# Dealing matmuls out between attention's last steps, a relu part on another engine, and the parts of x2 behind their transposes

## The chip, the core and the metric

The kernel runs on one core of a Trainium2 chip. The metric is the device time of one execution in microseconds (us), the median of several runs. A core has five engines, each with its own in-order queue: TensorE (PE: matmuls and transposes), VectorE (DVE), ScalarE (ACT), GpSimd (POOL) and SyncE (SP, which here only issues DMAs). An instruction that waits holds up all that stands behind it on its engine.

## The reference

Three stages in a row, attention with the 32 largest scores, a dense mixture of four experts, and a layer that takes the largest of three products:

```python
scores = q @ k.T / sqrt(64)                    # 2 batches x 8 heads, 576 x 576, float32
mask = scores >= 32nd largest of each row
x = softmax(where(mask, scores, -1e9)) @ v     # then heads side by side: 1152 x 512
p = domain_probs / (domain_probs.sum(-1) + 1e-9)
x = sum over e of p[:, e] * (relu(x @ w1[e]) @ w2[e])       # 4 experts, 512 -> 1024 -> 512
h = max(x @ m1, x @ m2, x @ m3)                # 512 -> 768, weights given as float64
out = h @ w_out                                # 768 -> 512, weights float64
```

## The kernel before

**Products.** A float32 product is made of three faster ones: each operand is split into a high and a low part (`whi`, `wlo` of a weight, `xh`, `xl` of x, `h` and its low part of a hidden layer, `x2h`, `x2l` of the experts' output), and `product` (L682 to L684) adds high by low, high by high and low by high. ACT makes the high part of a weight (L273), POOL or DVE the low part (L279). Tiles are 128 tokens, nine in all.

**Attention** runs in 36 pairs (two heads by 128 tokens), eight steps to a pair. DVE's search for the 32 largest sets its pace. Within a pair, PE transposes the probabilities (`psp`, L491 and L496), ACT copies them (`pt`, L494 and L499), PE multiplies them with v (`psv`, L533 and L536) and transposes the reciprocal sums (`psr`, L519). `attention()` is a generator: it emits one step and yields.

**Dealing out.** The loop at the end of the kernel takes the steps one by one. Each step raises `clock["dve"]` by the time that its DVE work is estimated at, and `clock["goal"]` follows. While `clock["pe"]` is below the goal, `advance()` emits a piece of the next product (`products()`). So products stand between the steps in as large a number as the estimates say. After the last step `attention()` goes on yielding empty steps, each worth `PAUSE` = 0.8, until all conversions are done.

**Conversions.** The float64 weights of the last layer are turned into float32 in 48 pieces (`to_float32`): SP loads a piece (L222), ACT does two operations (L239, L240), DVE three (L242, L244, L246), POOL one (L249), and ACT issues a DMA that writes it to DRAM (L255, tile `narrow`). One begins per two steps from step 306 on (`W_FROM`, `W_STEP`). Four pieces make one float32 weight, which SP loads later (L212, `raw<-narrow`).

**Experts** run in stages 0 to 8, each over two or three tiles and half of the experts' weights. For each expert half, `half1(c, i, u)` makes the hidden layer, and then `half2` of the half before multiplies it into the output. Stage 6 has tiles 5 and 6, stage 7 has 6, 7 and 8, stage 8 has 7 and 8. The evacuation of a hidden layer is the relu on ACT (L824) and the low part on DVE (L826); every fourth one (`ON_POOL_H`) is instead copied by ACT twice (L817, L818), with the low part on POOL (L819). Evacuations are not emitted at once: `later()` puts them on a list, whose next entry `tick()` emits at the next product, and `flush()` empties the list.

**The last layer** (`largest`) follows for three groups of three tiles. `turned` transposes a tile of the experts' output on PE (`pst`, L902), ACT makes `x2h` (L908) and DVE `x2l` (L909), two parts for each tile. Nine `c` products follow (three triples; the largest of a triple is collected in `tm`: L947 on ACT, L949 on DVE; its high part is `hh`, L952 on ACT), then the next group's transposes and the `d` products (`pso`). Hidden layers, `c` products and transposes share six PSUM banks in turn, so each waits until the bank's last tile is evacuated.

Of the kernel before, what the change touches and what calls it, by code (L numbers as in the profile page):

```python
# [24 lines left out]
ON_POOL_H = 4  # L25
# [4 lines left out]
PAUSE = 0.8  # L30
LATE = 7
# [29 lines left out]
def kernel(  # L61
# [41 lines left out]
    HALVES = [range(E) if not n % 2 else range(E, 2 * E) for n in range(len(STAGES))]  # L103
# [24 lines left out]
    clock = {"dve": 0.0, "pe": 0.0, "goal": AHEAD}  # L128
# [4 lines left out]
    def pe(n):  # L133
        clock["pe"] += n / 2400.0

    def bank(name):
        return pg.tile([P, 512], F32, tag="g", name=name)
# [147 lines left out]
    def weight(key, oldest=None):  # L285

        w_split_to(w_index[oldest or key] + W_AHEAD + 2 * whole(key))
        return w_hl[key]
# [90 lines left out]
    def xs_of(tiles):  # L379

        at_ = [place(t) for t in tiles]
        step = max(1, at_[-1] - at_[0]) // max(1, len(at_) - 1)
        assert at_ == list(range(at_[0], at_[-1] + 1, step))
        return [[x[:, a].rearrange("p (s n) -> p s n", n=P)[:, at_[0]:at_[-1] + 1:step] for a in range(KT)] for x in xring]
# [174 lines left out]
    def attention():  # L559

        NP = len(pairs)
# [76 lines left out]
        s = min(later)  # L638
        while s <= end:
            todo = later.pop(s, [])  # L640
            i = 0
            while i < len(todo):
                f, a = todo[i]
                f(*a)
                todo[i + 1:i + 1] = between.pop(s, [])
                todo += later.pop(s, [])
                i += 1
            yield s, [c for c in last if last[c] + (READY if c[1] == HP - 2 else 0) == s]
            s += 1

# [13 lines left out]
    def tick():  # L664
        for x in list(lag):
            x.pop(0)()
            if not x:
                lag.remove(x)

    def flush():  # L670
        while lag:
            tick()

    def later(*stages):
        tick()
        lag.append(list(stages))
# [37 lines left out]
    def hidden(N):  # L714
        if 2 * N <= 512:
            ht = hp_.tile([P, 2, 512], F32R, tag="h", bufs=4, name="h")
            return ht[:, 0, 0:2 * N], ht[:, 1, 0:2 * N]

        assert len(x_ready) == len(pairs) and 2 * N <= 2 * WIDTH
        hh = kv.tile([P, 2, S], F32R, tag="kT", bufs=5, name="hh")  # L720
        hl = hp_.tile([P, 2, 512], F32R, tag="h", bufs=4, name="hl")
        return [x.rearrange("p a n -> p (a n)")[:, 0:2 * N] for x in (hh, hl)]
# [68 lines left out]
    def experts():  # L791
        begin = {}

        def half1(c, i, u):
            tiles = STAGES[c]
            N = len(tiles) * P
            if c in WHOLE:
                ps = bank("ps1")
                w = weight((c, "a", i, u)).rearrange("p (a f) -> p a f", f=256)
                for f in range(2):  # L800
                    for a in range(KT):
                        pe(4 * P)
                        nc.tensor.matmul(ps[:, f * P:(f + 1) * P], lhsT=w[:, a, f * P:(f + 1) * P], rhs=xfull[:, a, :], start=f == a == 0, stop=f == 1 and a == KT - 1)
                    yield True
                h = hp_.tile([P, 2, 512], F32, tag="h", bufs=4, name="hfull")[:, 0, 0:2 * P]
                later(lambda: [nc.scalar.activation(out=h, in_=ps[:, 0:2 * P], func=AF.Relu), made.add(("h", c, i, u))])
                yield h
                return
            for groups in layer1(weight((c, "a", i, u)), xs_of(tiles), N, begin.pop((c, i, u), None)):
                if groups is None:  # L810
                    tick()
                    yield True
            hh, hl = hidden(N)
            count = made_h[0] = made_h[0] + 1
            if ON_POOL_H and not count % ON_POOL_H and (c, i) < (LATE - 1, HALVES[LATE - 1][-1]):
                raw = ms.tile([P, 2 * WIDTH], F32, tag="tm", bufs=2, name="raw")
                later(lambda: [nc.scalar.activation(out=raw[:, g], in_=ps, func=AF.Relu) for g, ps in groups],  # L817
                      lambda: [nc.scalar.activation(out=hh[:, 0:2 * N], in_=raw[:, 0:2 * N], func=AF.Copy),  # L818
                               nc.gpsimd.tensor_tensor(out=hl[:, 0:2 * N], in0=raw[:, 0:2 * N], in1=hh[:, 0:2 * N].bitcast(F32), op=ALU.subtract),  # L819
                               made.add(("h", c, i, u))])  # L820
                yield hh, hl
                return
            dve(2 * N)
            later(lambda: [nc.scalar.activation(out=hh[:, g], in_=ps, func=AF.Relu) for g, ps in groups],  # L824
                  *[lambda: None] * H_LAG,
                  lambda: [nc.vector.scalar_tensor_tensor(out=hl[:, g], in0=ps, scalar=0.0, in1=hh[:, g].bitcast(F32),  # L826
                                                          op0=ALU.max, op1=ALU.subtract) for g, ps in groups]
                  + [made.add(("h", c, i, u))])
            yield hh, hl

        outs = {}

        def half2(c, i, hs, ti):
            t = STAGES[c][ti]
            if not i % 2:
                outs[t] = po.tile([P, DM], F32, tag="o", name="ps2") if ti < 2 else bank("ps2")
            ps = outs[t]
            assert {("h", c, i, 0), ("h", c, i, 1)} <= made
            if c in WHOLE:
                for u in range(2):  # L840
                    w = weight((c, "b", i, u), (c, "b", i, 0)).rearrange("p (f n) -> p f n", f=2)
                    for f in range(2):
                        pe(4 * DM)
                        nc.tensor.matmul(ps, lhsT=hs[u][:, f * P:(f + 1) * P], rhs=w[:, f, :], start=not i % 2 and u == f == 0, stop=i % 2 == 1 and u == f == 1)
                        yield True
            else:
                yield from layer2(ps, [weight((c, "b", i, u), (c, "b", i, 0)) for u in range(2)], hs, len(STAGES[c]) * P, ti, not i % 2, i % 2 == 1)
            if not i % 2:
                return
            first = t not in accs  # L850
            if first:
                sums(t)
            later(*[lambda: None] * E_LAG, gated(ps, t, i // 2, first, c == LAST_IN[t] and i == HALVES[c][-1]))

        before = None
        for c in range(1, len(STAGES)):
            phase[0] = c
            newest = max(STAGES[c])
            if c == 1:
                i = HALVES[c][0]  # L860
                for parts in (range(HP - 2), (HP - 2,)):
                    while (newest, parts[-1]) not in x_ready:
                        yield None
                    for n, x in enumerate([(i, 0), (i, 1), (i + 1, 0), (i + 1, 1)]):
                        if not parts[0]:
                            begin[(c, *x)] = (po if n < 2 else pg).tile([P, 512], F32, tag="go"[n < 2], name="ps1")
                        yield from begun(begin[(c, *x)], weight((c, "a", *x), (c, "a", i, 0)), xs_of(STAGES[c]), 2 * P, parts)
                        flush()
            while (newest, HP - 1) not in x_ready:
                yield None  # L870
            for i in HALVES[c]:
                hs = []
                for u in range(2):
                    for y in half1(c, i, u):
                        if y is not True:
                            hs.append(y)
                        yield True
                if i == HALVES[c][-1]:
                    x_free.update(t for t in STAGES[c] if LAST_IN[t] == c)
                if before is not None:  # L880
                    for ti in range(len(STAGES[before[0]])):
                        yield from half2(*before, ti)
                before = c, i, hs
        flush()
        yield from turned_ahead(len(STAGES))
        for ti in range(len(STAGES[before[0]])):
            yield from half2(*before, ti)
        flush()
# [23 lines left out]
    def turned_ahead(n):  # L912

        if n < len(PHASES) and PHASES[n][0] == 2:
            c = PHASES[n][1]
            for ti in range(len(GROUPS[c])):
                turned(c, ti)
                yield True
# [163 lines left out]
```

## Time and profile before

| | us |
|---|---|
| median of 3 runs | 752.82 (751.12 to 754.62) |
| profiled execution | 751.61 |
| its span (what the trace covers) | 749.5 |
| around the span | 2.1 |
| PE busy | 721.0 |
| DVE busy | 586.7 |
| ACT busy | 505.2 |
| POOL busy | 474.7 |

The granted TensorE clock is at its full level over the whole span. Times in the rows below are us from the start of the span. In the trace attention ends at about 448, the experts at about 592, and the `c` products of the first group run from there to about 631.

### The profile page before, as it was taken

The numbers are of one execution on the slowest core, as the hardware profiler recorded it, in microseconds if no ns is written. First come the engines' busy times: TensorE is split into PE (matmuls) and PEld (weight loads), VectorE is DVE, ScalarE is ACT, GpSimd is POOL, SyncE is SP. The second block draws the span as 40 slices with busy tenths as digits, with TensorE's granted clock in tenths as the row PEclk, the third lists the DMA queues.
The fourth block names the chain that finished last, engine by engine and source line by source line (L and its number), as shares of the span: only waits on it lengthen the run. The fifth ranks groups of instructions, "written<-read, shape, count | busy, mean of one in ns | idle before, by whom it ended". The sixth has DMA issues, their size and how long they took to land. (4 is left out here: it accounts for less than half of the span.)

```text
span 749.5 us, 13764 instructions
## 1 busy us (share of the span) xinstructions
PE 721.0 (96%) x4758; PEld 641.2 (86%) x4758; DVE 586.7 (78%) x1171; ACT 505.2 (67%) x1132; POOL 474.7 (63%) x421
## 2 busy tenths in 40 slices
PE   6799999999999999999999998999999999999997
PEld 4587788888989989898989977899989899999996
DVE  6999989989999899999999965887688754233331
ACT  4668889899977787788797857666557533442531
POOL 2514778689979797697778659875655563442520
PEclk9999999999999999999999999999999999999999
DMA  7594565545647364445445355887879762453501
GB/s 220 179 267 160 154 179 160 156 127 162 190 123 214 109 189 125 148 134 154 142 125 152 126 183 160 299 297 269 293 230 343 245 194 73 153 170 101 195 1 42
DMA packets 56485, 130.15 MB, mean 174 GB/s; under 512 B 9760, under 2 KB 23328, under 8 KB 56416
## 3 DMA queue, kind: packets, MB, share of 16 engines
q1 hardware_dynamic: 48064, 120.69, 51.9%
q10 hardware_dynamic: 8352, 8.59, 3.2%
q8 instruction: 37, 0.61, 0.3%
q14 instruction: 32, 0.26, 0.1%
HBM read 120.60 MB, written 8.65 MB: 172 GB/s over the span
## 5 line engine op out<-in xcount | busy, mean ns | idle before, releaser
L279 POOL TENSOR_TENSOR wlo<-raw,whi 128x512 fp32r<-128x512 f32 x252 | 329.8, 1338 | 126.5 <-ACT whi L273 119.2
L273 ACT ACTIVATE whi<-raw 128x1024 fp32r<-128x1024 f32 x164 | 169.8, 1056 | 29.5 <-issue 9.4
L682 PE MATMUL ps<-xl,whi 128*128 128x256 f32 (+1 forms) x584 | 173.6, 297 | 1.2 <-DVE narrow L246 0.8
L684 PE MATMUL ps<-xh,wlo 128*128 128x256 f32 (+1 forms) x584 | 170.7, 292 | 0.0
L683 PE MATMUL ps<-xh,whi 128*128 128x256 f32 (+1 forms) x584 | 170.6, 292 | 0.0
L445 DVE MAX8 m<-work 128x8 f32<-128x576 f32 x216 | 155.0, 744 | 0.1
L682 PEld LDWEIGHTS ps<-xl,whi 128*128 128x128 f32 x584 | 110.8, 190 | 2.5 <-DVE narrow L246 1.1
L279 DVE TENSOR_TENSOR wlo<-raw,whi 128x1024 fp32r<-128x1024 f32 x38 | 60.4, 1590 | 64.8 <-ACT whi L273 51.9
L683 PEld LDWEIGHTS ps<-xh,whi 128*128 128x128 f32 x584 | 109.8, 188 | 0.8 <-issue 0.2
L684 PEld LDWEIGHTS ps<-xh,wlo 128*128 128x128 f32 x584 | 109.7, 188 | 0.0
L447 DVE MATCH_REPLACE8 work<-m,work 128x576 f32<-128x576 f32 x144 | 106.6, 741 | 0.0
L682 PE MATMUL ps<-wlo,h 128*128 128x512 f32 x224 | 91.0, 406 | 0.9 <-POOL wlo L279 0.9
L684 PE MATMUL ps<-whi,h 128*128 128x512 f32 x224 | 87.9, 393 | 3.6 <-POOL h L819 3.6
L683 PE MATMUL ps<-whi,h 128*128 128x512 f32 x224 | 87.8, 392 | 0.0
L249 POOL TENSOR_TENSOR narrow<-narrow,raw 128x256 int32<-128x256 int32 x48 | 42.2, 883 | 34.4 <-issue 13.0
L432 ACT ACTIVATE s<-pss 128x288 f32<-128x288 f32 x144 | 51.3, 399 | 11.5 <-PE pss L420 11.2
L445 DVE MAX8 m<-s 128x8 f32<-128x576 f32 x72 | 53.8, 747 | 4.7 <-ACT s L432 4.7
L684 PEld LDWEIGHTS ps<-whi,h 128*128 128x128 f32 x224 | 42.1, 188 | 13.9 <-POOL h L819 4.4
L447 DVE MATCH_REPLACE8 work<-m,s 128x576 f32<-128x576 f32 x72 | 53.3, 740 | 0.0
L682 PEld LDWEIGHTS ps<-wlo,h 128*128 128x128 f32 x224 | 42.9, 192 | 9.1 <-POOL wlo L279 2.7
L682 PE MATMUL ps<-x2l,whi 128*128 128x384 f32 x144 | 48.3, 336 | 1.3 <-DVE x2l L909 1.3
L684 PE MATMUL ps<-x2h,wlo 128*128 128x384 f32 x144 | 48.5, 337 | 0.0
(111 smaller groups left out, 1463.0 us busy)
## 6 DMA issues: line engine op xcount, KB each, us to landing
raw<-in_w_dram SPq DMA_DIRECT2D x128, 512.0 KB, 4.3
raw<-narrow SPq DMA_DIRECT2D x36, 512.0 KB, 3.9
raw<-in_m_dram SPq DMA_DIRECT2D x36, 256.0 KB, 4.8
whole<-in_w_dram SPq DMA_DIRECT2D x14, 512.0 KB, 6.1
narrow<-narrow ACTq DMA_DIRECT2D x48, 128.0 KB, 4.5
kraw<-in_k_dram SPq DMA_DIRECT2D x16, 288.0 KB, 4.5
qraw<-in_q_dram SPq DMA_DIRECT2D x48, 64.0 KB, 3.8
raw<-in_mo_dram SPq DMA_DIRECT2D x12, 256.0 KB, 5.1
```

Source lines behind the costliest of these rows:

```text
L249: nc.gpsimd.tensor_tensor(out=out.bitcast(I32), in0=out.bitcast(I32), in1=last, op=ALU.add)
L273: nc.scalar.activation(out=hi, in_=raw, func=AF.Copy)
L279: on.tensor_tensor(out=lo[:, x], in0=raw[:, x], in1=hi[:, x].bitcast(F32), op=ALU.subtract)
L432: nc.scalar.activation(out=s[:, h, :], in_=halves[h][:, 0:SH], func=AF.Copy)
L445: nc.vector.max(m[:, 8 * r:8 * r + 8], src)
L447: nc.vector.match_replace(out=self.w[j], in_to_replace=m[:, 8 * r:8 * r + 8], in_values=src, imm_value=NEG)
L682: nc.tensor.matmul(ps, lhsT=lh, rhs=rl, start=first, stop=False)
L683: nc.tensor.matmul(ps, lhsT=lh, rhs=rh, start=False, stop=False)
L684: nc.tensor.matmul(ps, lhsT=ll, rhs=rh, start=False, stop=last)
```

## The change

Three edits. In `attention()`, from step 291 on (8 steps by 36 pairs, and 2), each step raises the estimated DVE clock by `PAUSE` on top of its own work. The condition for a relu low part on POOL now leaves out the whole of stage 6 and what follows, where it left out only the last half of stage 6 and what follows. And `flush()` is called directly behind the transposes of the first group, ahead of the last `half2`.

```diff
@@ attention()
                 todo += later.pop(s, [])
                 i += 1
+            if s > 8 * NP + 2:
+                clock["dve"] += PAUSE
             yield s, [c for c in last if last[c] + (READY if c[1] == HP - 2 else 0) == s]
             s += 1
@@ half1(c, i, u)
             count = made_h[0] = made_h[0] + 1
-            if ON_POOL_H and not count % ON_POOL_H and (c, i) < (LATE - 1, HALVES[LATE - 1][-1]):
+            if ON_POOL_H and not count % ON_POOL_H and c < LATE - 1:
                 raw = ms.tile([P, 2 * WIDTH], F32, tag="tm", bufs=2, name="raw")
@@ experts()
         flush()
         yield from turned_ahead(len(STAGES))
+        flush()
         for ti in range(len(STAGES[before[0]])):
             yield from half2(*before, ti)
```

Line numbers behind the first edit grow by two, behind the third by three: L682 to L684 become L684 to L686, L826 becomes L828, L902, L908 and L909 become L905, L911 and L912, L947, L949 and L952 become L950, L952 and L955.

PE around the last pair's transposes and its products with v, before (`ps_6139` is an output of `half2`, `ps_6255` a hidden layer):

```order
L682 MATMUL ps_6139<-wlo,h 128x512
L683 MATMUL ps_6139<-whi,h 128x512
L684 MATMUL ps_6139<-whi,h 128x512
L491 MATMUL psp<-ident,p 128x128 x8
L496 MATMUL psp<-ident,p 128x128
L533 MATMUL psv<-pt_6196,v_last_112 128x128
L536 MATMUL psv<-pt,vt 64x128 x8
L519 MATMUL psr<-ident,rb 128x128
L682 MATMUL ps_6255<-xl,whi 128x256
```

The same place after (`ps_6230` is a hidden layer, `ps_6089` an output of `half2`):

```order
L684 MATMUL ps_6230<-xl,whi 128x256
L685 MATMUL ps_6230<-xh,whi 128x256
L686 MATMUL ps_6230<-xh,wlo 128x256
L533 MATMUL psv<-pt_6258,v_last_112 128x128
L536 MATMUL psv<-pt,vt 64x128 x8
L519 MATMUL psr<-ident,rb 128x128
L684 MATMUL ps_6089<-wlo,h 128x512
```

Between the last pair's transposes and its first product with v stood nothing; now 12 matmuls of the hidden layer `ps_6230` stand there.

ACT at the same place, before (`raw_6222` is a piece to convert, `ps_6055` the hidden layer whose low part POOL makes):

```order
L521 ACTIVATE r<-psr 128x128
L556 ACTIVATE xh<-xt 128x128
L504 ACTIVATE rs<-rs 128x2
L514 ACTIVATE rb<-rr 128x128
L494 ACTIVATE pt<-psp 128x512 x2
L499 ACTIVATE pt_6196<-psp 128x128
L521 ACTIVATE r<-psr 128x128
L556 ACTIVATE xh<-xt 128x128
L239 ACTIVATE psc<-raw_6222 128x256
L240 ACTIVATE raw_6222<-raw_6222 128x256
L273 ACTIVATE whi<-raw 128x1024 x2
L817 ACTIVATE raw<-ps_6055 128x512
```

And after:

```order
L521 ACTIVATE r<-psr 128x128
L273 ACTIVATE whi<-raw 128x1024 x2
L826 ACTIVATE h<-ps_6055 128x512
L556 ACTIVATE xh<-xt 128x128
L273 ACTIVATE whi<-raw 128x1024
L826 ACTIVATE h<-ps_6192 128x512
L504 ACTIVATE rs<-rs 128x2
L514 ACTIVATE rb<-rr 128x128
L494 ACTIVATE pt<-psp 128x512 x2
L499 ACTIVATE pt_6258<-psp 128x128
```

Three weight copies and two relu have come ahead of the copies of `pt`, and the conversion has gone behind them.

ACT where the last conversions are written out, in the first group's `c` products, before:

```order
L947 ACTIVATE tm<-ps_7979 128x384
L255 DMA narrow_106<-narrow 128x256
L239 ACTIVATE psc<-raw_7885 128x256
L240 ACTIVATE raw_7885<-raw_7885 128x256
L273 ACTIVATE whi<-raw 128x1024
L255 DMA narrow_107<-narrow 128x256
L239 ACTIVATE psc<-raw_7936 128x256
L240 ACTIVATE raw_7936<-raw_7936 128x256
L255 DMA narrow_107<-narrow 128x256
L273 ACTIVATE whi<-raw 128x1024
L255 DMA narrow_107<-narrow 128x256 x2
L952 ACTIVATE hh<-tm 128x768
```

And after (`ps_7979` above belongs to the first `c` product of the first triple, `ps_8199` and `ps_8216` to the first of the third):

```order
L255 DMA narrow_107<-narrow 128x256
L239 ACTIVATE psc<-raw_8074 128x256
L240 ACTIVATE raw_8074<-raw_8074 128x256
L273 ACTIVATE whi<-raw 128x1024
L255 DMA narrow_107<-narrow 128x256
L955 ACTIVATE hh<-tm 128x768
L273 ACTIVATE whi<-raw 128x1024
L950 ACTIVATE tm<-ps_8199 128x384
L950 ACTIVATE tm<-ps_8216 128x384
L255 DMA narrow_107<-narrow 128x256 x2
L273 ACTIVATE whi<-raw 128x1024
```

The last two writes stood ahead of the first triple's high part; now they stand behind the evacuations of the third triple's first product.

## Rows read from the trace of the kernel before

**Rows 1.** Page, busy time: engine, us, share of the span, instructions.

```profile
PE 721.0 (96%) x4758; PEld 641.2 (86%) x4758; DVE 586.7 (78%) x1171; ACT 505.2 (67%) x1132; POOL 474.7 (63%) x421
```

**Rows 2.** Waits of PE, 440 to 600 us: total, times, longest.

```profile
PE ps L684 <- POOL h L819: 2.3, 1, 2.3
...
PE ps L682 <- DVE narrow L246: 0.8, 1, 0.8
PE ps L682 <- POOL wlo L279: 0.3, 1, 0.3
```

**Rows 3.** Timeline of PE, last pair: start, us, instruction, count, [idle before, releaser].

```profile
442.96 0.39 PE L684 MATMUL ps<-whi,h 128*128 128x512 f32 x1
443.19 1.04 PE L491 MATMUL psp<-ident,p 128*128 128x128 f32 x8
...
445.78 0.49 PE L533 MATMUL psv<-pt,v_last 128*128 128x128 f32 x2 [1.44 <-ACT pt L499]
...
447.51 0.28 PE L683 MATMUL ps<-xh,whi 128*128 128x256 f32 x1
447.63 0.28 PE L684 MATMUL ps<-xh,wlo 128*128 128x256 f32 x1
```

**Rows 4.** Timeline of ACT, last pair.

```profile
444.50 1.06 ACT L494 ACTIVATE pt<-psp 128x512 f32<-128x512 f32 x2
445.45 0.28 ACT L499 ACTIVATE pt<-psp 128x128 f32<-128x128 f32 x1
...
449.15 1.99 ACT L273 ACTIVATE whi<-raw 128x1024 fp32r<-128x1024 f32 x2
```

**Rows 5.** Timeline of PE, second half of stage 6.

```profile
454.66 0.39 PE L683 MATMUL ps<-whi,h 128*128 128x512 f32 x1
...
457.33 0.50 PE L684 MATMUL ps<-whi,h 128*128 128x512 f32 x1 [2.28 <-POOL h L819]
457.67 0.39 PE L682 MATMUL ps<-wlo,h 128*128 128x512 f32 x1
```

**Rows 6.** Timeline of POOL ahead of that.

```profile
450.28 5.07 POOL L279 TENSOR_TENSOR wlo<-raw,whi 128x512 fp32r<-128x512 f32 x4 [1.13 <-ACT whi L273]
...
456.00 1.28 POOL L819 TENSOR_TENSOR h<-raw,h 128x512 fp32r<-128x512 f32 x1
```

**Rows 7.** Timeline of DVE, three places.

```profile
469.97 4.45 DVE L279 TENSOR_TENSOR wlo<-raw,whi 128x1024 fp32r<-128x1024 f32 x1 [2.92 <-ACT whi L273]
...
591.96 1.41 DVE L909 TENSOR_TENSOR x2l<-pst,x2h 128x384 fp32r<-128x384 f32 x4
...
615.32 1.23 DVE L279 TENSOR_TENSOR wlo<-raw,whi 128x1024 fp32r<-128x1024 f32 x1 [0.34 <-ACT whi L273]
```

**Rows 8.** Timeline of PE, from the first group's transposes to the second's.

```profile
584.91 1.47 PE L902 MATMUL pst<-ident,acc 128*128 128x128 f32 x12
...
591.49 0.39 PE L684 MATMUL ps<-whi,h 128*128 128x512 f32 x1
593.23 0.45 PE L682 MATMUL ps<-x2l,whi 128*128 128x384 f32 x1 [1.35 <-DVE x2l L909]
...
630.79 1.47 PE L902 MATMUL pst<-ident,acc 128*128 128x128 f32 x12
```

**Rows 9.** Timeline of ACT (ACTq: its DMA issues), in the first `c` products.

```profile
605.27 0.33 ACTq L255 DMA_DIRECT2D narrow<-narrow  x1
...
622.67 0.49 ACT L947 ACTIVATE tm<-ps 128x384 f32<-128x384 f32 x1 [1.40 <-PE ps L684]
```

**Rows 10.** Timeline of SP's DMA issues, the same stretch.

```profile
609.58 1.41 SPq L212 DMA_DIRECT2D raw<-narrow  x2
```

**Rows 11.** DMA issues, 610 to 640 us: count, KB each, median us to landing.

```profile
raw<-narrow SPq DMA_DIRECT2D x6, 512.0 KB, 3.4
```

**Rows 12.** Line L255 over the whole span: a write's us to landing.

```profile
DMA to landing us min/median/max: 1.8/4.5/7.5
```

**Rows 13.** Line L212 over the whole span: a weight load's us to landing.

```profile
DMA to landing us min/median/max: 3.1/4.3/9.0
```

## Prediction

> **What bounds the kernel now.** I read the page's busy times first: TensorE (PE) is busy for 721.0 of 749.5 us [rows 1], so the time is PE's work plus the holes in it. The diff leaves PE's matmuls and transposes as many as they are, so only holes can move. The view of PE's waits over the stretch that the diff touches, 440 to 600 us, is next: it has five holes, of which [rows 2] show three; the two others carry their idle time in brackets in the timelines [rows 3, 8]. One rule of reading: ends of matmuls are modelled, so a hole is measured from start to start. A 128x512 matmul hands over after 0.23 us (442.96 to 443.19 [rows 3]).
>
> - Last pair of attention: nine transposes start at 443.19, the first product with v (psv, L533) at 445.78 [rows 3]. The nine take 1.0 us, so 1.6 us are empty: psv needs `pt`, whose last copy ACT starts at 445.45 [rows 4]. Every product that was dealt out to these steps was used up by then.
> - Tile 6's relu low part on POOL: 454.66 to 457.33 [rows 5], less 0.23: 2.44 us. POOL's subtraction L819 starts at 456.00, behind four weight halves that began at 450.28 [rows 6].
> - Two short ones: 0.8 behind a conversion on DVE, 0.3 behind a weight half on POOL [rows 2].
> - Before the first product of x2: 591.49 to 593.23 [rows 8], less 0.23: 1.51 us. Four of the six low parts of x2 run on DVE only from 591.96 on [rows 7], since they are emitted between conversions and weight splits.
>
> After a long hole the next matmul also comes 0.34 instead of 0.23 us later (457.33 to 457.67 [rows 5]): 0.11 for each of three, 0.3 together. All that the change can win in this stretch is 1.6 + 2.44 + 0.8 + 0.3 + 1.51 + 0.3 = **7.0 us**.
>
> **Edit 1, products between the last steps.** 14 steps (291 to 304) raise the estimated DVE clock by 0.8 each, 11.2 estimated us. By the order, 12 instead of 6 products of 512 columns stand between the transposes and the psv of pair 34, 36 matmuls of 128x256 behind it, and 12 more between the transposes and the psv of pair 35. A 128x256 one takes 0.12 us (447.51 to 447.63 [rows 3]). The psv of pair 34 began at 440.2 and so begins 6 x 0.23 = 1.4 us later, at about 441.4 (some 0.2 were empty ahead of it). Its block with the first matmul behind it takes 1.73 (445.78 to 447.51 [rows 3]), 35 x 0.12 = 4.2 more bring PE to 447.2, nine transposes to 448.2, and 12 x 0.12 to **449.6**, where the psv of pair 35 stands. Its `pt` can be copied from 448.2: 1.06 for two and 0.28 for the last [rows 4] make 449.5. Ahead of that on ACT now stand three weight copies (two take 1.99 [rows 4]) and two relu, the last of a product that ends at 447.2, and two short steps of the row sums; I leave 0.2 us of this hole. Its bounds are 0 and the whole 1.6.
>
> The products that are moved ahead move the conversions behind them (one begins per two steps from step 306): each stands some five conversions later against the products, its load on SP, its parts on ACT, DVE and POOL, and its write on ACT. In stages 6 and 7 that is relief: the weight halves on POOL and the copies on ACT no longer stand behind them, which takes the 0.3. The 0.8 was due to a conversion on DVE and, ahead of it, a weight subtraction of 4.45 us at 469.97, which elsewhere takes 1.23 [rows 7]. Now the conversions are gone from there, but a slow subtraction would still stand ahead of the low part that frees the bank; I leave 0.3 of the 0.8, bounds 0 and 1.1. How late the conversions now end is the subject of the new wait below.
>
> **Edit 2, low part from POOL to VectorE.** By the order this is one instance, the h of stage 6's second half: two ACT copies and POOL's L819 (1.28 us [rows 6]) go; one ACT copy and one subtraction on DVE come, for which I take POOL's 1.28 at most. It is emitted with the last pair's steps, so it is done at about 446.5, and PE comes to it at about 452.8. The 2.44 goes. The cover is those 6 us; without it the edit would cost DVE's 1.28 at most.
>
> **Edit 3, x2 at once.** The six parts on ACT and six on DVE follow the transposes directly. On DVE four take 1.41 [rows 7], six 2.1; with ACT one part ahead, ACT's parts for the first and a conversion of about 0.8 on ACT between, I work out 3.9 us from the transposes' start. PE comes to x2 6.8 us after it (584.91 to 591.49 and 0.23 more [rows 8]). They are put ahead of the copy and the split of the first `c` weight on ACT and POOL, whose second half is ready at 8.05 and needed at 8.2. So the 1.51 goes, and its restart; at worst some 0.3 stays.
>
> Together the holes give back 7.0 - 0.2 - 0.3 = **6.5 us**.
>
> **A wait that is new.** Each conversion ends with a write to DRAM that ACT issues (L255), and SP then loads the float32 weight from there (L212). Before, the last write is issued at 605.27 [rows 9], 12.0 us after the start S = 593.23 of the `c` products [rows 8]. Now the last two stand on ACT behind the second evacuation of the seventh `c` product, which ran at 622.67 [rows 9], S + 29.4; so I take them at S + 29.9. The chain from there: write to SP's load 4.3 (605.27 [rows 9] to 609.58 [rows 10]), load 3.4 [rows 11], ACT's copy 1.1, DVE's subtraction 1.2 (615.32 [rows 7]): **S + 40.0** with 0.1 of issue. DVE is in order, and the evacuation of the eighth `c` product (0.55) stands behind that subtraction. The third transpose tile of x takes the bank of that product. PE is through the nine products at S + 37.6 (593.23 to 630.79 [rows 8]) and two transpose tiles later, at S + 38.4, it waits: to 40.6, so 2.2, with the restart **2.3 us**. Behind it nothing further is late: by the same working the last high and low part of the maximum come 0.9 and 0.4 us before PE. Bounds: write 1.8 to 7.5 [rows 12], load 3.1 to 9.0 [rows 13], which make the wait 0 to about 11.
>
> **Sum.** 6.5 - 2.3 = 4.2 us gained in the profiled execution (749.5 of span and 2.1 around it, 751.6 in all): 747.4. The median of the three runs is 752.82, 1.2 over it; against that I forecast **748.6 us**, a gain of 0.56%. About 0.5% (3.8 us) is what a measurement of this kernel can tell from no change; the borders are 749.1 and 756.6.
>
> **Rivals.**
> (a) Write and load are short: with a write of 1.8 [rows 12] the chain is 2.5 shorter, the new wait is 0, and 6.5 us are won: 746.3. For it: PE needs the result only 2.2 us earlier than I have it. Against: the median of such writes is 4.5 [rows 12].
> (b) Write or load is long: with a write of 7.5 [rows 12] the new wait is 5.5, the gain 1.0, the time 751.8. For it: the two last writes are issued back to back, and SP's load of that weight waits for both. Against: the last write before took 4.3.
> (c) Edit 1 does not do what it says: it fills PE, but ACT's copies of weights ahead of `pt` take as long as the products, so the 1.6 stays; and the subtraction on DVE runs at its 4.45 us [rows 7], so the 0.8 stays as well. Gain 4.2 - 1.4 - 0.5 = 2.3: 750.5. For it: 449.6 against 449.5 has no room, and the row of 4.45 lies exactly there. Against: that row's subtraction will start at another time against POOL's work.
> The Trainium skill, page "SBUF — State Buffer", section "Who interferes with whom", has a rule for such a row: a VectorE instruction with two SBUF inputs contends with a GpSimd one that reads SBUF, by a lock under which one of them stands still. A duration of 4.45 against 1.23 for the same shape agrees in kind, though the row alone does not show what held it. By that rule alone the 0.8 would stay, and the sum would be 749.1. The moved relu part reads one input from PSUM, so the rule does not speak against edit 2.
> (d) Slower. The chain of write, load, copy and subtraction takes its worst, 7.5 + 9.0 [rows 12, 13] instead of 4.3 + 3.4, 8.8 more: the wait is 11.1, and 6.5 - 11.1 is a loss of 4.6: 757.4. It decides from a chain that is 8 us longer than mine. Against it: those are the longest of the whole trace, and both would have to come together.
>
> **How the numbers follow.** Forecast 0.45, (a) 0.18, (b) 0.18, (c) 0.14, (d) 0.05. The forecast lies 0.5 us inside the border of "faster"; for the scatter of its terms I count 0.08 of its 0.45 as "same", and 0.02 of (c) as faster. Faster: 0.45 - 0.08 + 0.18 + 0.02 = 0.57. Slower: 0.05. Same: 0.38. The range takes in the forecast, (a) with 0.8 us of scatter, (c) and most of (b): 745.5 to 752.0.
>
> **What would show it.** In the profile of the changed kernel: no wait of psv on `pt` over 0.3 us and none on a POOL relu part (else edits 1 and 2 are misjudged); no wait of x2's first product on its low part (L912); a new wait of 1 to 4 us of the transposes (L905) on DVE's evacuation L952 about 38 us after the first `c` product, with ACT waiting for the load of the last float32 weight right before it. If that wait is missing, (a) holds; if it is over 5 us, (b) or (d). The forecast is wrong altogether if holes turn up between 482 and 584, where there are none now, or if conversions that end later leave an earlier `c` product without its weight.

## The result, and the profile after

| | before | after |
|---|---|---|
| median, us | 752.91 (751.12 to 754.62, 4 runs) | 743.21 (742.43 to 746.91, 4 runs) |
| profiled execution, us | 751.61 | 743.31 |
| its span, us | 749.5 | 740.8 |

The ratio is 0.9881 (95% interval 0.9841 to 0.9921): 9.7 us or 1.2% less, where I forecast 4.2 and a time of 748.6 with a range from 745.5. In the two profiled executions it is 8.3 us; the other 1.4 come from medians that lie elsewhere than the profiled executions (1.3 above it before, 0.1 below it after). The spans differ by 8.7, since after has 2.5 us around its span and not 2.1.

PE has the same 4758 instructions; its busy time, in which the ends of matmuls are modelled, is 2.6 us shorter than in [rows 1], and the busy share rises because the span is shorter:

```profile
PE 718.4 (97%) x4758; PEld 641.4 (87%) x4758; DVE 582.6 (79%) x1172; ACT 504.9 (68%) x1131; POOL 474.2 (64%) x420
```

The view of PE's waits from 430 us to the end has no row at all, where [rows 2] and the timelines had five. The timeline of PE at the last pair (start, us, instruction), to be read against [rows 3]:

```profile
446.61 1.04 PE L491 MATMUL psp<-ident,p 128*128 128x128 f32 x8
...
448.89 0.28 PE L686 MATMUL ps<-xh,wlo 128*128 128x256 f32 x1
449.01 0.38 PE L533 MATMUL psv<-pt,v_last 128*128 128x128 f32 x2
```

The psv of the last pair follows the matmul ahead of it after 0.12 us. ACT and DVE there, to be read against [rows 4]: the last copy of `pt`, and the relu low part that was on POOL.

```profile
448.50 0.28 ACT L499 ACTIVATE pt<-psp 128x128 f32<-128x128 f32 x1
```

```profile
445.49 0.69 DVE L828 SCALAR_TENSOR_TENSOR h<-ps,h 128x512 fp32r<-128x512 f32 x1 [2.09 <-ACT h L826]
```

`pt` is done at 448.8, 0.2 us ahead of PE; the low part at 446.2. At x2 DVE has the six low parts done at 581.9, and the first product follows its predecessor with no gap (against [rows 7, 8]):

```profile
580.51 1.42 DVE L912 TENSOR_TENSOR x2l<-pst,x2h 128x384 fp32r<-128x384 f32 x4 [0.44 <-ACT x2h L911]
```

```profile
584.56 0.39 PE L686 MATMUL ps<-whi,h 128*128 128x512 f32 x1
584.79 0.34 PE L684 MATMUL ps<-x2l,whi 128*128 128x384 f32 x1
```

Now the wait that I had added to the sum. With S = 584.79 the chain of the last conversions reads, on ACT, SP and DVE (ACTq and SPq are their DMA issues), against [rows 9, 10]:

```profile
614.12 0.49 ACT L950 ACTIVATE tm<-ps 128x384 f32<-128x384 f32 x1 [0.95 <-PE ps L686]
614.12 0.81 ACTq L255 DMA_DIRECT2D narrow<-narrow  x2
620.31 1.06 ACT L273 ACTIVATE whi<-raw 128x1024 fp32r<-128x1024 f32 x1 [5.70 <-DMA raw<-narrow]
```

```profile
616.51 1.28 SPq L212 DMA_DIRECT2D raw<-narrow  x3
```

```profile
621.46 1.23 DVE L279 TENSOR_TENSOR wlo<-raw,whi 128x1024 fp32r<-128x1024 f32 x1 [10.49 <-ACT whi L273]
622.60 1.95 DVE L952 TENSOR_TENSOR tm<-ps,tm 128x384 f32<-128x384 f32 x4
```

And the two writes among the DMA issues of 614 to 615 us (count, KB each, us to landing):

```profile
narrow<-narrow ACTq DMA_DIRECT2D x2, 128.0 KB, 1.9
```

The two writes are issued from S + 29.3 on, the last about where I had it (S + 29.9), but they land in 1.9 us instead of 4.3. SP's load follows at 616.51, its weight is there at 620.31 (3.8 us), copy and subtraction end at 622.7, and the first evacuation of the four frees its bank at 622.60 + 0.55 = 623.15. PE begins the twelve transposes at 622.24; at 0.11 us each the third tile of four would begin at 623.1. It begins at 623.2, so the wait is there, but with 0.1 us, and 0.06 behind it, it is too short for the list of waits. It shows in the duration of the twelve transposes, against 1.47 in [rows 8]:

```profile
622.24 1.63 PE L905 MATMUL pst<-ident,acc 128*128 128x128 f32 x12
```

### The profile page after: what moved, and what is told of

It is laid out like the page before. It is cut to its first block, busy times and chain, and to the rows that moved or that the text cites. A ratio compares the mean times of both kernels' runs of the same rounds, so it can differ in the third digit from the quotient of the medians.

```text
span 740.8 us, 13773 instructions
## 1 busy us (share of the span) xinstructions
PE 718.4 (97%) x4758; PEld 641.4 (87%) x4758; DVE 582.6 (79%) x1172; ACT 504.9 (68%) x1131; POOL 474.2 (64%) x420
## 4 chain that ended last, share of the span: by engine, by line
PE 69%; DVE 15%; ACT 9%; issue 3%; POOL 2%; DMA 1%; ACTq 0%; POOLq 0%
PE ps L684 17%; PE ps L686 17%; PE ps L685 17%; DVE m L445 7%; DVE work L447 6%; PE psv L536 3%; ACT whi L273 3%; PE pss L425 2%; PE psp L491 2%; POOL wlo L279 2%; PE pso L684 2%; PE psa L769 2%; PE pso L685 2%; PE pso L686 2%; PE pss L420 1%
## 5 line engine op out<-in xcount | busy, mean ns | idle before, releaser
L684 PE MATMUL ps<-xl,whi 128*128 128x256 f32 (+1 forms) x584 | 173.5, 297 | 0.4 <-POOL xl L557 0.4
L686 PE MATMUL ps<-xh,wlo 128*128 128x256 f32 (+1 forms) x584 | 170.7, 292 | 0.0
L684 PEld LDWEIGHTS ps<-xl,whi 128*128 128x128 f32 x584 | 110.7, 190 | 1.4 <-POOL xl L557 0.6
L686 PEld LDWEIGHTS ps<-xh,wlo 128*128 128x128 f32 x584 | 109.6, 188 | 0.0
L279 DVE TENSOR_TENSOR wlo<-raw,whi 128x1024 fp32r<-128x1024 f32 x38 | 55.7, 1468 | 68.6 <-ACT whi L273 56.7
L684 PE MATMUL ps<-wlo,h 128*128 128x512 f32 x224 | 90.8, 405 | 0.6 <-POOL wlo L279 0.6
L686 PE MATMUL ps<-whi,h 128*128 128x512 f32 x224 | 87.8, 392 | 1.3 <-POOL h L821 1.3
L249 POOL TENSOR_TENSOR narrow<-narrow,raw 128x256 int32<-128x256 int32 x48 | 45.0, 940 | 30.7 <-issue 10.2
L686 PEld LDWEIGHTS ps<-whi,h 128*128 128x128 f32 x224 | 42.1, 188 | 11.2 <-POOL h L821 1.7
L684 PEld LDWEIGHTS ps<-wlo,h 128*128 128x128 f32 x224 | 42.9, 192 | 8.2 <-POOL wlo L279 1.6
L686 PE MATMUL ps<-x2h,wlo 128*128 128x384 f32 x144 | 48.5, 337 | 0.0
L685 PE MATMUL ps<-x2h,whi 128*128 128x384 f32 x144 | 48.3, 336 | 0.0
```

The source lines that it names most:

```text
L249: nc.gpsimd.tensor_tensor(out=out.bitcast(I32), in0=out.bitcast(I32), in1=last, op=ALU.add)
L279: on.tensor_tensor(out=lo[:, x], in0=raw[:, x], in1=hi[:, x].bitcast(F32), op=ALU.subtract)
L684: nc.tensor.matmul(ps, lhsT=lh, rhs=rl, start=first, stop=False)
L685: nc.tensor.matmul(ps, lhsT=lh, rhs=rh, start=False, stop=False)
L686: nc.tensor.matmul(ps, lhsT=ll, rhs=rh, start=False, stop=last)
```

## The experiments

All ran in groups beside the kernel before on the same chip; the medians of before in the four groups are 751.21, 750.49, 751.02 and 751.28. Three kernels hold one edit each, three hold two. Their diffs are the hunks of the change.

### One edit at a time

> Edit 1 alone (products dealt out between the last steps). Theory A, each edit takes its own holes: the holes at psv (1.9 us by starts), at the weight half on POOL (0.8) and at the narrow tile (1.05) go, the POOL relu part (2.55) and x2 (1.5) stay: 3.7 us less than before, span about 745.8. Theory B, the relu part on POOL was late only because conversions and weight halves stood ahead of it there, which edit 1 moves away: its hole goes too, 6.2 us less, span about 743.3, and only the x2 wait of 1.3 to 1.5 is left after 430 us.

> Edit 2 alone (one relu low part on VectorE instead of POOL). Theories A and B alike: the hole of 2.5 us before the second half of stage 6 goes, all other holes of before stay: span about 747.0. If the low part on DVE gets caught behind the conversions there, a hole of up to 1 us stays in its place and the span is 747 to 748.

> Edit 3 alone (parts of x2 behind their transposes). Both theories: the x2 hole of 1.5 us goes and nothing else moves: span about 748.0. If the copy of the first c weight, which now stands behind x2's parts, is late instead, part of the 1.5 stays as a wait on its low part on POOL.

> All three edits, beside the others on one chip: 8.2 us less than before in the trace (span about 741), no wait of PE after 430 us. The last two writes take about 2 us because the DMA engines are idle there, so the transposes wait for nothing.

| kernel | median | span | ratio to before |
|---|---|---|---|
| edit 1 | 743.98 | 741.9 | 0.9905 (0.9891 to 0.9919) |
| edit 2 | 750.44 | 748.8 | 0.9991 (0.9978 to 1.0004) |
| edit 3 | 750.06 | 747.3 | 0.9989 (0.9978 to 1.0000) |
| all | 742.96 | 740.6 | 0.9892 (0.9880 to 0.9905) |

Edit 1 alone gives 7.2 of the 8.25 us, edits 2 and 3 alone less than they take in holes. Theory B's result came: with edit 1 alone the relu part is still on POOL, and the only wait of PE between 430 and 640 us is x2's.

```profile
PE ps L684 <- DVE x2l L911: 0.7, 1, 0.7
```

On POOL of that kernel the low part runs at 447.76, 8.2 us earlier than in [rows 6]. The four weight halves still stand ahead of it, but they start 7.5 us earlier, and the conversion between them and the low part is gone:

```profile
442.77 5.06 POOL L279 TENSOR_TENSOR wlo<-raw,whi 128x512 fp32r<-128x512 f32 x4 [3.37 <-ACT whi L273]
447.76 1.30 POOL L821 TENSOR_TENSOR h<-raw,h 128x512 fp32r<-128x512 f32 x1
```

With edit 2 alone its 2.4 us hole is gone, but the waits of PE from 430 to 640 us are these, and one of 0.2 us of psp on DVE's `p`:

```profile
PE psv L533 <- ACT pt L499: 1.5, 1, 1.5
PE ps L682 <- DVE narrow L246: 0.9, 1, 0.9
PE ps L682 <- DVE x2l L909: 0.7, 1, 0.7
PE ps L682 <- POOL wlo L279: 0.6, 2, 0.3
```

The weight half on POOL now holds PE up twice in place of once. And something else took time there. The windows of that kernel (us, PE busy and count, granted clock, DMA share, GB/s) behind the psv hole:

```profile
446.00:447.00 1.00, 1.00 (x10) 0.72 0.95 389
447.00:448.00 1.00, 1.00 (x12) 0.50 0.24 82
448.00:449.00 1.00, 1.00 (x7) 0.50 0.00 0
449.00:450.00 1.00, 1.00 (x7) 0.57 0.00 0
```

The granted clock falls to 0.50 (1.2 of 2.4 GHz) for some 3.4 us after PE has stood idle for 1.5. In the profile of before the same hole is followed by a clock of 1.00. The price, from the starts in the timelines: the psv block took 2.3 us (445.87 to 448.20) instead of 1.5, and the next eight matmuls 0.2 each instead of 0.12, together some 1.4 us.

### Pairs of edits

> Edits 1 and 3 without 2: the relu low part stays on POOL. If edit 1 alone empties POOL's queue ahead of it (theory B), edit 2 is worth nothing beside it: span within 0.3 of that with all three (740.6), no wait after 430 us. If edits add up (theory A): a hole of 2.5 us is back, span 743.

> Edits 1 and 2 without 3: the parts of x2 stay between the conversions. Theory: the wait of x2's first product, 0.9 us with edit 1 alone, is what edit 3 is worth beside edit 1: span 741.5 to 742, that one wait after 430 us. Rival: with edit 2 DVE has one instruction more ahead and the wait is the 1.5 of before, span 742.2.

> Edits 2 and 3 without 1: the holes at psv (1.6 and 0.3), at the weight halves on POOL (0.5 to 1.2) and at the narrow tile (1.0) stay, the POOL relu part and x2 are gone: 4 us of the 8.2, span about 745 to 746, and 1.5 us more in executions in which the clock drops behind the psv hole. Rival (the holes share one cause, the conversions that stand too early): those two edits alone leave over 5 us of holes, as the single ones did, span 746.5 or more.

| kernel | median | span | ratio to before |
|---|---|---|---|
| edits 1 and 3 | 742.80 | 740.6 | 0.9891 (0.9876 to 0.9906) |
| edits 1 and 2 | 746.55 | 744.2 | 0.9940 (0.9923 to 0.9957) |
| edits 2 and 3 | 749.96 | 747.8 | 0.9981 (0.9971 to 0.9990) |

Without edit 2 nothing is missing: the same span, no wait of PE. Beside edit 1 it is worth nothing that can be measured.

Without edit 3 I was wrong by 2 us. The wait of x2's first product is not 0.7 but 2.7 (waits of PE, edits 1 and 2):

```profile
PE ps L684 <- DVE x2l L911: 2.7, 1, 2.7
```

DVE of that kernel shows why: between the first pair of low parts and the second stand a weight split, which waits 2.33 us for ACT's copy, and a conversion, and a second conversion stands between the second pair and the last.

```profile
581.42 1.47 DVE L279 TENSOR_TENSOR wlo<-raw,whi 128x1024 fp32r<-128x1024 f32 x1 [2.33 <-ACT whi L273]
...
584.06 0.75 DVE L911 TENSOR_TENSOR x2l<-pst,x2h 128x384 fp32r<-128x384 f32 x2
...
585.97 0.75 DVE L911 TENSOR_TENSOR x2l<-pst,x2h 128x384 fp32r<-128x384 f32 x2
```

With edit 1 alone one conversion stands among the parts of x2, not two, the last pair runs at 585.26 and the wait is 0.7. The two kernels differ by edit 2 alone, one low part moved to another engine; by which path that moves a conversion among the parts of x2 is not shown. So edit 3 is worth 1.3 us of span beside edit 1 (741.9 to 740.6), and 3.6 beside edits 1 and 2 (744.2 to 740.6), of which 1.5 are again a clock of 0.50 behind the hole.

Without edit 1 the two others leave, by starts, holes of 4.2 us, as expected (psv 1.7, weight halves 1.3, the narrow tile 1.0, 0.2 more), and a clock drop behind psv; together about 6 of the 7.2 us to the kernel with all three. The span of 747.8 is 2 over what I had expected; both numbers that I put on this run were too coarse to decide between its theories, and the last us is not accounted for.

### The wait that did not come

Three kernels put something ahead of the last two writes, two move the conversions.

> All three edits, and ten extra DMA writes of 192 KB each (2 MB, of a tile to scratch memory that nothing reads) issued by SP just as the last two conversions are written out. Theory T, a write lands in 2 us only because the DMA engines are idle there and takes 4 or more under load: the last write and load together take 3 to 5 us longer, the chain that I forecast is the late one, PE waits 2 to 5 us at the third transpose tile for L952's evacuation, span 743 to 746. Theory F, the landing is a property of this transfer and not of the load: it stays at 2 us, no wait over 0.5, span 740.6 to 741.2.

```diff
                         if i == 0:
                             nc.scalar.activation(out=tm[:, g], in_=ps, func=AF.Copy)
+                            if c == 0 and j == 2 and not g.start:
+                                for y in range(10):
+                                    nc.sync.dma_start(out=scratch[y], in_=tm[:, g])
```

Median 746.52, span 744.0, and the wait is there:

```profile
PE pst L906 <- DVE tm L956: 2.6, 1, 2.6
```

But the write is not late, as theory T had it. The DMA issues show that the two conversion writes landed in 2.3 us at full DMA load, and SP's timeline that SP itself was late: ten issues took it 5 us, to 617.16, and the load of the last weight stands right behind them, at 617.26 where the changed kernel has 616.51, though the writes were issued 1 us earlier here. That load then took 4.7 us (617.26 to ACT's copy at 621.93) instead of 3.8.

```profile
narrow<-narrow ACTq DMA_DIRECT2D x2, 128.0 KB, 2.3
```

```profile
612.11 5.05 SPq L954 DMA_DIRECT2D scratch<-tm  x10
617.26 2.88 SPq L213 DMA_DIRECT2D raw<-narrow  x5
```

So a full load of the DMA engines with small writes does not make this write late; it made the weight's load late. The next kernel put writes ahead of it on its own queue.

> All three edits, and four extra writes of 192 KB on ACT's own queue directly ahead of the last two conversion writes. Theory Q, a write's landing is set by what was issued ahead of it (3 writes in 2.5 us and weight loads in before, nothing in the changed kernel): the last write lands 1.4 us later for the issues and takes 3.5 to 4.5 in place of 1.9; the chain is some 3.5 us longer and PE waits 3 to 4 us at the third transpose tile, span 744 to 745. Theory F, 2 us whatever is ahead: only the issues count, a wait of 1 to 1.5 us, span about 742.

```diff
+        if n == WIDE * len(wide) - 2:
+            for to in scratch:
+                nc.scalar.dma_start(out=to, in_=last_tm[-1][:, 0:384])
         nc.scalar.dma_start(out=narrow[wide[n // WIDE][0]][:, n % WIDE ...
```

Median 744.06, span 741.6. Theory F: four writes of 192 KB ahead, and the two land in 1.9 us. Issuing four DMAs puts 1.9 us on the chain (613.28 to 615.20), the weight's load is 0.5 shorter than in the changed kernel, and PE waits 1.5 us:

```profile
scratch<-tm ACTq DMA_DIRECT2D x4, 192.0 KB, 2.0
narrow<-narrow ACTq DMA_DIRECT2D x2, 128.0 KB, 1.9
```

```profile
PE pst L910 <- DVE tm L958: 1.5, 1, 1.5
```

In the kernel before, SP had issued two loads of 512 KB (at 601.13 and 602.21, median 4.2 us to landing) shortly ahead of the last write at 605.27. Large transfers on SP's queue were the last candidate.

> All three edits, and three extra copies of 512 KB from memory to memory (float32 weights, to a place that nothing reads) issued by SP about 1.5 us before the last two conversion writes, behind one small write that gives the time. Theory L, a write lands late where large transfers were issued shortly ahead of it on SP's queue: the two writes land in 4 us or more in place of 1.9, the chain is 2 to 4 us longer, PE waits 2 to 4 us at the third transpose tile, span 743 to 745. Theory F, this write lands in about 2 us whatever else is under way, and the 4.2 of before has another cause: wait under 1 us, span 740.6 to 741.6.

```diff
                         if i == 0:
                             nc.scalar.activation(out=tm[:, g], in_=ps, func=AF.Copy)
+                            if c == 0 and j == 2 and not g.start:
+                                nc.sync.dma_start(out=scratch, in_=tm[:, 0:16])
+                                for y in range(3):
+                                    nc.sync.dma_start(out=loads[y], in_=narrow[0, y])
```

Median 748.71, span 746.2. Theory L: the DMA issues around 613 us and the wait.

```profile
loads<-narrow SPq DMA_DIRECT2D x3, 512.0 KB, 5.4
narrow<-narrow ACTq DMA_DIRECT2D x2, 128.0 KB, 5.4
```

```profile
PE pst L907 <- DVE tm L958: 3.9, 1, 3.9
```

The same two writes, at the same place, land in 5.4 us (the median of 4.4 and 6.4) behind three copies of 512 KB. The chain is as I had forecast it; the wait is 3.9 us, and the clock of 0.50 behind that hole (626 to 631 us) costs some 2.5 more, while up to the hole this execution was 1.1 us ahead. So large transfers ahead on another queue make this write late.

Whether this is what made it 4.2 us in the kernel before can be read in that kernel's trace. Its DMA packets by queue (q1 is SP's, q10 ACT's, q8 loads instructions; packets, MB, share of 16 engines) in three windows, 602.8 to 605.2, 607 to 608 and 608 to 609:

```profile
q1 hardware_dynamic: 205, 0.77, 96.5%
q10 hardware_dynamic: 5, 0.01, 0.6%
...
q8 instruction: 1, 0.02, 5.5%
...
q10 hardware_dynamic: 7, 0.01, 4.5%
```

ACT had issued the first of its last three writes at 602.82, but until 605.2 almost nothing of its queue moved beside SP's loads. That is a wait like the one in loads_ahead, though these packets are of 3.8 KB, and the last write stood behind the two that they held. The rest is another thing: by 607.6 all but seven packets were through, and these ran one after another from 608 to 609, behind a single packet of instructions that took 0.9 us (5.5% of 16 engines for 1 us). The second profile of before and edit 3 alone have such a packet at this place too, and a last write of 4.4 us. That the seven waited for that packet is an inference from the order; no run takes it away.

> All three edits, conversions begin at step 314 in place of 306. By the order the very last write then stands on ACT behind the copies of two transpose tiles, some 10 us later. Theory: the chain write 2, load 3.8, copy 1.1, subtraction 1.2 ends at about S + 47.8 (S the first c product), the first d product that needs it stands at S + 41.7: a new wait of 5 to 7 us, span 746 to 748. Rival: another of the four writes or a second raw buffer covers it and the wait is under 2.

```diff
-WIDE, W_FROM, W_STEP = 4, 306, 2
+WIDE, W_FROM, W_STEP = 4, 314, 2
```

Median 749.59, span 748.7. The wait came where it was worked out and a little shorter than the 5 to 7 us, 4.7 us at the first `d` product that needs the last weight, with 2.6 us more in thirteen matmuls at a clock of 0.50 behind it (631.33 to 637.03, 0.43 each instead of 0.23):

```profile
PE pso L684 <- DVE wlo L279: 4.7, 1, 4.7
```

> All three edits, conversions begin at step 302 in place of 306, two earlier. Theory: the place of the conversions against the products matters only where an in-order queue stands ahead of PE; two conversions more ahead of stage 7 bring back at most the short wait behind a narrow tile (0 to 1 us): span 740.6 to 741.6. Rival, every conversion ahead of the last pair's end costs what before's did (0.3 to 1 each): 742 to 743.

`W_FROM` 302 in place of 306: median 743.34, span 741.1, no wait of PE after 430 us. Two conversions earlier cost and win nothing that can be measured.

### A second profile of before

> The kernel before once more, for a second profile of it. If the clock drop seen behind holes of 1.7, 2.6, 2.6 and 4.9 us in four other kernels is chance from execution to execution, this profile has it behind one of its holes or not, with the same holes (1.6, 2.4, 1.0, 1.5) and a span of 749 to 751.5; without holes of its own making it would show a granted clock of 1.0 throughout.

Span 748.7, with the clock at 0.50 behind the hole of the POOL relu part. Its windows:

```profile
456.00:457.00 1.00, 0.48 (x1) 0.66 0.72 94
457.00:458.00 1.00, 1.00 (x4) 0.50 0.80 249
458.00:459.00 1.00, 1.00 (x4) 0.50 1.03 411
```

The same program, the same 2.4 us hole as in [rows 5], once with the clock at 1.00 behind it and once not. Yet this execution was not the longer one: PE was slower there by 1.7 us, the weight half and the conversion that held it up later, 0.7 each by starts, were ready in time, and what is left is inside the scatter from 0 to 430 us.

## Why the prediction was wrong, point by point

**What bounds the kernel: right.** PE's instructions did not change, only holes did; all but 0.3 us (below) lay where the views showed them.

**The holes: right in kind, under-counted by 1.3 us.** From start to start, with the 0.26 us taken off that the two executions differ by at 427 us, the stretch gave back:

| hole | worked out to go | measured |
|---|---|---|
| last pair (psv 34 and 35) | 1.4, and 0.1 restart | 2.4 |
| POOL relu part | 2.4, and 0.1 restart | 2.5 |
| weight half on POOL | 0.3 | 0.8 |
| narrow tile on DVE | 0.5 | 1.0 |
| x2 | 1.5, and 0.1 restart | 1.6 |
| sum | 6.5 with the restarts | 8.3 |

Less the 0.15 that the transposes wait, that is 8.15. Two steps failed. I broke my own rule and took the two short holes by their idle entries (0.8 and 0.3 [rows 2]), where starts give 1.05 and 0.8: matmuls around a hole also come late by 0.1 each without an entry. And the psv of pair 34 had 0.3 us empty that I named as "some 0.2" and left out of the sum. Both are in the timeline and in no wait. The nine transposes also hand over after 0.9 us and not 1.0, which makes the hole of pair 35 1.7; and 0.15 of the 2.4 is no hole: the 36 matmuls of 128x256 start every 0.113 us there, where later ones take 0.118.

**Residuals: wrong, 0.5 us too careful.** I left 0.2 at psv and 0.3 at the narrow tile. `pt` was ready 0.2 us ahead of PE: I had the second relu on ACT wait for a product that ends at 447.2, but by the order the bank of that product is full after 24 of the 36 matmuls, so ACT came to the row sums sooner, and PE too was 0.6 us earlier than I had it. At the narrow tile I had the wrong instruction in view: PE waited there for the conversion itself, whose `psc` takes one of the same six banks, and between the subtraction of 4.45 us [rows 7] and that conversion stood a second one of 2.06. The same two take 2.98 and 1.52 us in the changed kernel and start 2.8 and 3.8 us earlier against PE's work.

**Edit 1 "takes" 1.6, 0.3 and 0.5, edit 2 the 2.44, edit 3 the 1.51: wrong as a split.** The sum needed no split, so this cost nothing; but a reader who had dropped edit 1 would have lost 7.2 us and not 2.2. Edit 1 acts on all five holes at once: it puts products into the psv hole, and on ACT and POOL it brings weight copies and relu ahead of the last pair's `pt` and puts the conversions behind. How much of the 7.2 us is the conversions' share is not shown, since no run moves them alone in the kernel before; beginning them two conversions earlier cost nothing (earlier4), and the psv hole had no conversion ahead of it (the order of ACT before).

**The new wait: the step that failed most, 2.3 us forecast and 0.15 measured.** Order, place and engine were as worked out: the writes behind the evacuation of the seventh `c` product, DVE's evacuation behind the subtraction, the bank of the third transpose tile. The term that was mis-sized is the write: 4.3 from [rows 9, 10], measured 1.9, while the load took 3.8 instead of 3.4. I had taken the nearest row in time; I should have asked what else the DMA engines were doing in that row. Two loads of 512 KB had been issued 3 and 4 us ahead of it, two writes stood before it on its queue, and its last packets came behind a load of instructions; at S + 29 SP has nothing left to issue until this very write lands. Rival (a) named the 1.8 and got 0.18; three experiments show that the wait is there as soon as the chain is late, be it by the write (loads_ahead) or by the issues ahead of it and the load (ahead4, traffic).

**The rivals.** (a) came, with 746.3 too high by the holes under-counted, the residuals and the scatter of the median. (b) did not come by itself; loads_ahead forced its long write (6.4 us for the last one), with a median of 748.7. (d) did not come. (c) did not come. The row of 4.45 is the first weight subtraction on DVE. In the changed kernel that one takes 2.98 us. In both it ends 1.1 us after the end of a run of GpSimd instructions (474.42 behind 473.34, and 464.23 behind 463.15). The next one on DVE took 2.06 us before and takes 1.52 now; the GpSimd one that starts 0.4 us behind it takes 2.28 instead of the 1.31 of a neighbour. The Trainium skill, page "SBUF — State Buffer", section "Who interferes with whom", says that the ports that the two share are an exclusive lock. These rows agree with that. Which of the two stands still they leave open: at both places a GpSimd conversion was still running when VectorE started; at 469.97 VectorE was 0.1 us ahead of GpSimd's next instruction and lost, at 467.18 it was 0.4 us ahead and won.

The kernel before, DVE and POOL:

```profile
476.84 2.06 DVE L279 TENSOR_TENSOR wlo<-raw,whi 128x1024 fp32r<-128x1024 f32 x1
470.07 2.56 POOL L279 TENSOR_TENSOR wlo<-raw,whi 128x512 fp32r<-128x512 f32 x2
472.57 0.77 POOL L249 TENSOR_TENSOR narrow<-narrow,raw 128x256 int32<-128x256 int32 x1
```

The changed kernel, DVE and POOL:

```profile
461.25 2.98 DVE L279 TENSOR_TENSOR wlo<-raw,whi 128x1024 fp32r<-128x1024 f32 x1 [0.90 <-ACT whi L273]
467.18 1.52 DVE L279 TENSOR_TENSOR wlo<-raw,whi 128x1024 fp32r<-128x1024 f32 x1 [0.44 <-ACT whi L273]
```

```profile
462.40 0.75 POOL L249 TENSOR_TENSOR narrow<-narrow,raw 128x256 int32<-128x256 int32 x1
467.58 2.28 POOL L279 TENSOR_TENSOR wlo<-raw,whi 128x512 fp32r<-128x512 f32 x1
...
471.78 1.31 POOL L279 TENSOR_TENSOR wlo<-raw,whi 128x512 fp32r<-128x512 f32 x1
```

**The numbers.** 4.2 forecast, 2.15 for the wait that all but stayed away, 1.8 for holes and residuals: 8.15 in the stretch, and 8.3 measured from profile to profile. The last 1.4 to 9.7 are the medians: the forecast set out from a median of three runs, 752.82, where the four larger groups have 750.5 to 751.3, and in the group with all three edits the gain is 8.25. The range reached down to 745.5; with rival (a), every hole counted by starts, nothing left of them and the same 0.8 of scatter it would have reached 743.7, still above the 743.21.

## What to carry to other kernels

Count holes from start to start over the whole stretch, and against the regular spacing; a list of waits leaves out the late matmuls around them. If several engines hold PE up in one stretch, look for what an edit moves on all of them before sharing the gain out among edits: here the one that changes the order on all was worth 7.2 us, and the two edits aimed at single holes 1.0 together beside it. The duration of a DMA belongs to what is under way around it, so look at the queues and packets of the new place before carrying it over from the old.

## What the runs showed of the hardware that I had not expected

- **A hole can cost more than itself.** Behind holes of PE of 1.5 us (edit 2 alone, edits 2 and 3), 2.4 (edit 3 alone, the second profile of before), 2.6, 2.7, 3.9 and 4.7 us the granted clock fell to 0.50, for 3.4 or 6.8 us, at 1.4 to 2.6 us of PE's time; behind the same 1.4 and 2.3 us holes in the first profile of before, and behind the 1.5 of ahead4, it stayed at 1.00. Behind the 2.4 us hole of one and the same program it goes from execution to execution. It fits the scatter: the runs of kernels without a long hole lie within 0.3 to 1.2 us (edit 1: 743.86 to 744.13; all three: 742.76 to 743.25; edits 1 and 3: 742.71 to 743.87), with the exception of one run of 746.91 of the changed kernel in its first group; those with one lie within 2.1 to 6.9 us (ahead4: 743.79 to 745.89; edit 2: 748.95 to 754.40; traffic: 744.20 to 751.07). That the clock makes this scatter is an inference; a profile was taken of one execution each.
- **A small write lands in 1.8 to 2.3 us next to other small writes, and in 4.4 and 6.4 behind copies of 512 KB**, though the copies were on another queue (SP's). The sizes of the packets differ; that they are the cause is not shown. The 14 packets of copies that begin from 613.4 to 614 move 0.46 MB, 33 KB each, and take 289.5% of the 16 engines' 0.6 us, which is 2.0 us each; beside the ten writes 269 packets move 0.38 MB in 1 us, 1.4 KB each. The share of a window counts a packet's whole time where it begins, so 1.75 and then 0.17 does not say that the engines were idle from 614 to 615:

```profile
613.00:614.00 1.00, 1.00 1.75 460
614.00:615.00 1.00, 1.00 0.17 66
```
